# Score products of a windowed attention, in tiles of 104 and 64 key columns

## The chip, the cores and the metric

The kernel runs on one core of a Trainium2 chip. The time is the device time of one execution in microseconds (us); of several timed executions the median is given. The profile is of one execution more, taken by the hardware profiler.

## The reference

Four batches, eight heads, 768 positions and a head width of 64. Each position attends to the 96 positions up to and including itself and to the first 8 positions of its sequence, with a bias that falls with distance, by a slope of the head's own. The 512 numbers that the heads give for a position go through two projections to 1536, whose products are projected back to 512.

```python
scores = scale * np.matmul(q, k.transpose(0, 1, 3, 2))
rel = pos[:, None] - pos[None, :]
keep = (pos[None, :] < n_global) | ((rel >= 0) & (rel < n_local))   # 8 and 96
scores = np.where(keep, scores + bias, -1e9)
a = softmax(scores)                       # float32, as everything here
x = np.matmul(a, v)                       # then (B * S, H * D) = (3072, 512)
return ((x @ w_a) * (x @ w_b)) @ w_out    # (512, 1536) twice, (1536, 512)
```

## The kernel before, in words

**Tiling.** The 3072 rows are cut into six units of 512 rows (four blocks of 128 queries). Attention of a unit is done in four granules, each with four entries of two heads by one block. So there are 24 granules. `granule_ops` (line 547) does one: it loads `qk`, which holds queries and keys of the granule with the head's 64 numbers on the partitions, head 0 on partitions 0 to 63 and head 1 on 64 to 127, and does two rounds of two entries each. A round is one call of `scores` (line 574). It fills two PSUM banks, `ps[0]` for head 0 and `ps[1]` for head 1, with 2 x 168 columns: for each of the two entries 128 queries by 168 keys.

**Which keys.** The 128 queries of a block are taken as two halves, s = 0 and s = 1, of 64. For an entry the keys lie in `qk` as 232 columns (`KB`): columns 0 to 63 are positions -96 to -33 from the block's start, 64 to 159 are -32 to 63, 160 to 167 are the eight first positions of the sequence, and 168 to 231 are 64 to 127. Both halves need columns 64 to 167: that is 104 (`KX`). Half 0 also needs columns 0 to 63, and half 1 also 168 to 231. So each half has 168 keys (`KW`), of which the 104 shared ones come first in PSUM.

**The score products.** A matmul here has 64 partitions of input (one head's width) and 64 output lanes (one half), so it uses a quarter of TensorE's array. `tile_position=(64 * h, 64 * s)` says which: the head picks the rows, the half the columns. In the kernel before, `scores` issues for each entry, in this order and each for head 0 and then head 1: half 1 with all of its 168 columns (64 to 231 lie in a row), half 0 with the 104 shared ones, and half 0 with its own 64. These are six matmuls an entry, twelve a round, all recorded at line 581. The operands are float32.

**What follows a round.** For each entry and head VectorE adds the mask and takes the row's minimum (line 602), ScalarE takes the exponential and the sum (line 619), then come the division, the transposes and, a granule or so later, the value products (`values`, line 695, matmuls at line 701, `pa`). In three of the six units the values of a granule are computed during the next granule.

**The projections.** These are the bulk of TensorE's work: `product` and `plain_product` (lines 922 and 943, banks `al` and `ga`) and `back` (line 1099, banks `acc0` to `acc3`), with 512- or 256-column matmuls on the whole array, each product in three parts of a split of the numbers. Weights come in as 64-bit words and are converted on the chip (`to32`, line 351). The projections run over passes, a set of weights by a unit; the attention of later units is spread over the passes of earlier ones (`SPANS`, line 58).

**What sets the order.** Every piece of work is an `Op` with a due time and a cost for each engine that can do it. `Schedule.order` (line 176) walks through them like a list scheduler and fixes, before the program runs, the order of the instructions on every engine and of the transfers on SyncE's queue. A round of score products is one such `Op`, with a cost of 720 ns on TensorE (`pe=720`, line 591); what is due at its side is interleaved with it round by round, and not inside a round. Waits are between whole buffers: the mask operations of a round wait for the last matmul into their bank.

Of the kernel before, what the change touches and what calls it, by code (L numbers as in the profile page):

```python
# [34 lines left out]
KX = 96 + NG  # L35
KW = KX + 64
# [60 lines left out]
QUADS1 = (28400.0, 31000.0, 36000.0, 35540.0, 46130.0, 44380.0)  # L97
QUADS2 = (48000.0, 51000.0, 54000.0, 51210.0, 58890.0, 63000.0)
GAP = 20220.0


def entry(u, g, i):
    if u:
        return g, i
    return 2 * (g % 2) + i // 2, 2 * (g // 2) + i % 2
# [51 lines left out]
class Schedule:  # L157
# [14 lines left out]
    def op(self, due, emit, reads=(), writes=(), late=0.0, port=(), **costs):  # L172

        self.ops.append(Op(len(self.ops), due, costs, emit, reads, writes, late, port))
# [95 lines left out]
def act(n, psum=False):  # L270
    return (51 if psum else 93) + 0.833 * n


def dve(n, fast=False):
    return 67 + (0.523 if fast else 1.045) * n
# [14 lines left out]
class Fast:  # L290
# [256 lines left out]
    def granule_ops(self, u, p, due, x, d, before):  # L547
        nc, op = self.nc, self.plan.op
        n = f"{u}_{p}"
        g = self.granule  # L550
        self.granule += 1
        px, py = self.px[g % PTBUFS], self.py[g % PTBUFS]
        qk = self.kept("qk%d" % (g % KBUFS), "qk" + n)
        vt = self.sbuf([P, VN], F32, "vt", "vt" + n, VBUFS)
        if g >= KBUFS:
            self.dma(
                due - LOADLEAD,
                lambda: qk[:, :],
                lambda: self.a["qk"][u, p],
                [],  # L560
                [qk],
                (QN + KN) * 4 * P,
            )
        self.dma(
            due + VLAG - 4000.0, lambda: vt[:, :], lambda: self.a["vd"][u, p], [], [vt], VN * 4 * P
        )
        t = self.sbuf([P, NH, 2, KW], F32, "t", "t" + n, TBUFS)
        sm = self.sbuf([P, 4, 2 * NH], F32, "sm", "sm" + n, 3)
        for r in range(2):
            self.count += 1  # L570
            tags = self.early_bank("psS", u, p, self.count)
            ps = [self.bank(tags[h], f"ps{n}_{r}_{h}") for h in range(2)]

            def scores(e, r=r, ps=ps):
                for b in range(2):
                    i = 2 * r + b
                    q0, k0, c0 = i * P, QN + i * KB, b * KW
                    for s, c, k, w in ((1, 0, 64, KW), (0, 0, 64, KX), (0, KX, 0, 64)):
                        for h in range(2):
                            rows = slice(64 * h, 64 * h + 64)  # L580
                            nc.tensor.matmul(  # L581
                                ps[h][64 * s : 64 * s + 64, c0 + c : c0 + c + w],
                                qk[rows, q0 + 64 * s : q0 + 64 * s + 64],
                                qk[rows, k0 + k : k0 + k + w],
                                start=True,
                                stop=True,
                                skip_group_check=True,
                                tile_position=(64 * h, 64 * s),
                            )

            op(due, scores, [qk], ps, pe=720)
            for b in range(2):
                i = 2 * r + b
                pair, blk = entry(u, p, i)
                kind = 0 if (4 * u + blk) % NB == 0 else 1
                for h in range(2):
                    j = 2 * i + h
                    w = slice(b * KW, b * KW + KW)
                    op(
                        due,  # L600
                        lambda e, i=i, w=w, h=h, b=ps[h], j=j, kind=kind, pair=pair: (
                            nc.vector.tensor_tensor_reduce(  # L602
                                t[:, i, h],
                                b[:, w],
                                self.mask[pair][:, h, kind],
                                -0.125,
                                3.0e38,
                                ALU.add,
                                ALU.min,
                                sm[:, 0, j : j + 1],  # L610
                            )
                        ),
                        [ps[h], (self.mask[pair], h)],
                        [(t, j), (sm, j)],
                        dve=dve(KW) + 10,
                    )
                    op(
                        due,
                        lambda e, i=i, h=h, j=j: nc.scalar.activation(  # L619
                            t[:, i, h],  # L620
                            t[:, i, h],
                            AF.Exp,
                            bias=sm[:, 0, j : j + 1],
                            scale=-1.0,
                            accum_out=sm[:, 1, j : j + 1],
                        ),
                        [],
                        [(t, j), (sm, j)],
                        act=act(KW) + 200,
                    )  # L630
        if before:
            before()
        tt = None
        if u not in DIRECT:
            tt = self.sbuf([P, 6, 2 * NH * 32], F32, "tt", "tt" + n, TTBUFS)
        for half in range(2):
            js = range(4 * half, 4 * half + 4)
            jw = slice(4 * half, 4 * half + 4)
            op(
                due,  # L640
                lambda e, jw=jw: nc.vector.tensor_scalar_add(sm[:, 2, jw], sm[:, 1, jw], 1e-9),
                [(sm, j) for j in js],
                [(sm, ("d", half))],
                dve=70,
            )
            op(
                due,
                lambda e, jw=jw: nc.vector.reciprocal(sm[:, 3, jw], sm[:, 2, jw]),
                [(sm, ("d", half))],
                [(sm, ("r", half))],  # L650
                dve=80,
            )
            flat = lambda: t[:, :].rearrange("p a b c -> p (a b) c")

            def norm(e, js=js, jw=jw):
                if e == "act":
                    for j in js:
                        nc.scalar.mul(flat()[:, j], flat()[:, j], sm[:, 3, j : j + 1])  # L658
                else:
                    for j in js:  # L660
                        nc.vector.tensor_scalar(
                            flat()[:, j], flat()[:, j], sm[:, 3, j : j + 1], None, op0=ALU.mult
                        )

            ts = [(t, j) for j in js]
            op(due, norm, [(sm, ("r", half))], ts, port=BOTH, dve=4 * dve(KW, True), act=4 * (act(KW) + 100))

            if u in DIRECT:
                for i in range(2 * half, 2 * half + 2):
                    self.direct(u, p, n, i, due, t, px, py)  # L670
                continue

            def turn(e, half=half):
                dst = tt[:, :].rearrange("p e (j k) -> p j e k", k=32)[:, 4 * half : 4 * half + 4]
                src = t[:, 2 * half : 2 * half + 2].rearrange("p a b c -> p (a b) c")
                for e0, c0, n in ((0, 0, 4), (4, KX, 2)):
                    nc.vector.transpose(  # L677
                        dst[:, :, e0 : e0 + n],
                        src[:, :, c0 : c0 + 32 * n].rearrange("p j (e k) -> p j e k", e=n),
                    )  # L680

            op(due, turn, ts, [(tt, half)], dve=dve(512) + dve(256))
        if u not in DIRECT:
            self.carry(n, due, tt, px, py)

        def late():
            self.values(u, p, due, vt, px, py, x, d)

        return late
# [478 lines left out]
    def run(self):  # L1168
# [31 lines left out]
        for i, (stay, u) in enumerate(PASSES):  # L1200
# [27 lines left out]
            for k, fp in enumerate(fps):  # L1228
                due = t + k * (times[i + 1] - t) / len(fps)
                if not i:  # L1230
                    due = [h + k * GAP for h in (HALF0, HALF1)]
                parts = (self.project_plain if plain else self.project)(i, fp, due, xf[u])
# [369 lines left out]
```

## Time and profile before

| | |
|---|---|
| median of 3 timed runs | 725.11 us |
| lowest and highest | 724.22 and 725.52 us |
| the profiled execution's own time | 728.68 us |
| its span, from first to last instruction | 726.4 us |
| mean granted clock of TensorE | 0.987 |
| VectorE busy | 578.9 us (80%) |
| ScalarE busy | 387.7 us (53%) |
| VectorE, mask operation of line 602 | 192 of 326 ns |
| HBM read and written | 110.45 and 50.86 MB |

How to read the profile: PE is TensorE's products, PEld its weight loads, which run beside products; DVE is VectorE, ACT is ScalarE, SPq the queue of SyncE that issues transfers. Busy time of a group of instructions is the time in which at least one of them ran, so that four matmuls on four quarters of the array count once. A product's record begins where it may start and ends, by a model, when its last result has left the array; records of neighbours therefore overlap. The mean of one at line 581 is 278 ns, while 1152 of them take 43.6 us together. A float32 matmul of the scores or the values leaves two records of products and two of weight loads.

### The profile page before, as it was taken

The numbers are of one execution on the slowest core, as the hardware profiler recorded it, in microseconds if no ns is written. First come the engines' busy times: TensorE is split into PE (matmuls) and PEld (weight loads), VectorE is DVE, ScalarE is ACT, GpSimd is POOL, SyncE is SP. The second block draws the span as 40 slices with busy tenths as digits, with TensorE's granted clock in tenths as the row PEclk, the third lists the DMA queues.
The fourth block names the chain that finished last, engine by engine and source line by source line (L and its number), as shares of the span: only waits on it lengthen the run. The fifth ranks groups of instructions, "written<-read, shape, count | busy, mean of one in ns | idle before, by whom it ended". The sixth has DMA issues, their size and how long they took to land.

```text
span 726.4 us, 15134 instructions
## 1 busy us (share of the span) xinstructions
PE 693.5 (95%) x5584; PEld 605.8 (83%) x5584; DVE 578.9 (80%) x1544; ACT 387.7 (53%) x989; POOL 1.8 (0%) x8
## 2 busy tenths in 40 slices
PE   5698998999999999999999999999999999999996
PEld 4487887777777788788899899899989999999995
DVE  7999997777687785799989898999999557746652
ACT  5987775745465673746455545666343434434310
POOL 1000000000000000000000000000000000000000
PEclk9799999999999999999999999999999999999999
DMA  8547998897989897776676888756794423343221
GB/s 296 213 163 259 269 294 300 267 305 250 304 280 303 253 335 247 262 266 228 221 249 232 294 259 301 245 201 230 233 337 151 146 59 102 131 145 102 74 73 62
DMA packets 67906, 162.39 MB, mean 224 GB/s; under 512 B 8432, under 2 KB 21872, under 8 KB 66032
## 3 DMA queue, kind: packets, MB, share of 16 engines
q1 hardware_dynamic: 67824, 161.34, 66.8%
q8 instruction: 46, 0.75, 0.4%
q14 instruction: 36, 0.29, 0.1%
HBM read 110.45 MB, written 50.86 MB: 222 GB/s over the span
## 4 chain that ended last, share of the span: by engine, by line
PE 68%; DMA 12%; DVE 11%; ACT 5%; issue 2%; SPq 1%; DVEq 0%; ACTq 0%
PE acc L1099 19%; PE al L922 16%; PE ga L922 12%; DMA wr<-wts 8%; PE ps L581 4%; PE pa L701 3%; ACT t L619 1%; DMA py<-mir 1%; DVE tt L677 1%; DMA X<-dx 1%; DVE t L602 1%; DVE wm L394 1%; ACT wm L369 1%; DVE wm L411 1%; SPq L323 1%
## 5 line engine op out<-in xcount | busy, mean ns | idle before, releaser
L1099 PE MATMUL acc<-w_O,hh 128*128 128x512 f32 x576 | 196.6, 400 | 0.0
L1099 PEld LDWEIGHTS acc<-w_O,hh 128*128 128x128 f32 x576 | 108.4, 188 | 25.1 <-issue 1.7
L1099 PE MATMUL acc<-w_O,hl 128*128 128x512 f32 x288 | 113.8, 395 | 0.4 <-DVE hl L342 0.3
L619 ACT ACTIVATE t<-t,sm 128x168 f32<-128x168 f32 x192 | 81.1, 424 | 20.2 <-DVE sm L602 20.0
L922 PE MATMUL al<-xf_T,w_S 128*128 128x256 f32 x576 | 76.8, 283 | 0.0
L922 PEld LDWEIGHTS al<-xf_T,w_S 128*128 128x128 f32 x576 | 72.2, 189 | 0.5
L332 ACT CAST hh<-h 128x512 fp32r<-128x512 f32 (+1 forms) x62 | 36.6, 592 | 50.2 <-DVE h L342 22.5
L1099 PEld LDWEIGHTS acc<-w_O,hl 128*128 128x128 f32 x288 | 54.3, 188 | 10.5 <-DVE hl L342 1.1
L581 PEld LDWEIGHTS ps<-qk 64*64 64x64 f32 x1152 | 36.3, 142 | 28.1 <-issue 14.2
L602 DVE CUSTOM_DVE_ANT_0 t<-ps,mask 128x168 f32<-128x168 f32 x192 | 53.3, 326 | 6.1 <-PE ps L581 5.6
L581 PE MATMUL ps<-qk 64*64 64x168 f32 (+2 forms) x1152 | 43.6, 278 | 14.4 <-DMA qk<-qk 7.0
L332 ACT COPY s<-al 128x512 f32<-128x512 f32 x47 | 27.5, 585 | 52.2 <-PE al L922 52.2
L369 ACT ACTIVATE wm<-wr 128x512 f32<-128x512 f32 x54 | 36.2, 670 | 34.7 <-DMA wr<-wts 25.2
L342 DVE TENSOR_TENSOR hl<-h,hh 128x512 fp32r<-128x512 f32 (+1 forms) x78 | 49.8, 642 | 5.2 <-ACT hh L332 4.9
L1031 DVE TENSOR_TENSOR s<-ga,s 128x512 f32<-128x512 f32 x48 | 32.8, 683 | 16.2 <-PE ga L922 16.0
L677 DVE STREAM_TRANSPOSE tt<-t 128x512 f32<-128x512 f32 x80 | 41.1, 552 | 0.8 <-ACT t L658 0.4
L404 ACT ACTIVATE wr<-wr 128x512 int32<-128x512 uint32 x54 | 36.2, 673 | 7.2 <-DMA wr<-wts 4.3
L701 PE MATMUL pa<-px,vt 104*64 104x128 f32 x384 | 38.9, 278 | 1.2 <-DMA px<-mir 1.2
L922 PE MATMUL ga<-xf_B,w_S 128*128 128x256 f32 x288 | 38.6, 283 | 1.3 <-ACT s L332 1.3
L922 PEld LDWEIGHTS al<-xf_B,w_A 128*128 128x128 f32 x288 | 37.5, 189 | 2.3 <-issue 0.3
L922 PE MATMUL ga<-xf_T,w_S 128*128 128x256 f32 x288 | 38.6, 283 | 0.6 <-DVE s L1031 0.5
L701 PE MATMUL pa<-py,vt 128*64 128x128 f32 x384 | 38.0, 273 | 1.1 <-DMA py<-mir 1.0
(274 smaller groups left out, 1318.6 us busy)
## 6 DMA issues: line engine op xcount, KB each, us to landing
wr<-wts SPq DMA_DIRECT2D x54, 512.0 KB
qk<-qk SPq DMA_DIRECT2D x24, 720.0 KB
mir<-tt SPq DMA_DIRECT2D x20, 768.0 KB
vt<-vd SPq DMA_DIRECT2D x24, 512.0 KB
X<-dx SPq DMA_DIRECT2D x10, 1024.0 KB
part<-o SPq DMA_DIRECT2D x32, 256.0 KB
wl_S<-dw_S SPq DMA_DIRECT2D x32, 256.0 KB
px<-mir SPq DMA_DIRECT2D x60, 128.0 KB
```

Source lines behind the costliest of these rows:

```text
L332: self.nc.scalar.copy(out(), src())
L342: lambda e: self.nc.vector.tensor_tensor(out(), a(), b(), op=op),
L369: lambda e: nc.scalar.activation(m(), high().bitcast(F32), AF.Abs),
L404: lambda e: nc.scalar.activation(low(), low().bitcast(U32), AF.Copy, scale=2.0**-29),
L581: nc.tensor.matmul(ps[h][64 * s : 64 * s + 64, c0 + c : c0 + c + w], qk[rows, q0 + 64 * s : q0 + 64 * s + 64], qk[rows, k0 + k : k0 + k + ...
L602: nc.vector.tensor_tensor_reduce(t[:, i, h], b[:, w], self.mask[pair][:, h, kind], -0.125, 3.0e38, ALU.add, ALU.min, sm[:, 0, j : j + 1],)
L619: lambda e, i=i, h=h, j=j: nc.scalar.activation(t[:, i, h], t[:, i, h], AF.Exp, bias=sm[:, 0, j : j + 1], scale=-1.0, accum_out=sm[:, 1, j ...
L677: nc.vector.transpose(dst[:, :, e0 : e0 + n], src[:, :, c0 : c0 + 32 * n].rearrange("p j (e k) -> p j e k", e=n),)
L701: nc.tensor.matmul(pa[64 * h : 64 * h + 64, i * P : i * P + P], vt[:lanes, v0 : v0 + 64], k[:, :, 2 * i + h], start=c == 0, stop=c == 1, s ...
L922: self.nc.tensor.matmul(bank[:, ab * HT : ab * HT + HT], w[:, a, (2 * ab + c) * P : (2 * ab + c) * P + P], x[:, b, c], start=first, stop=F ...
L1031: lambda e: nc.vector.tensor_tensor(s[:, :], bank[:, :], s[:, :], op=ALU.add),
L1099: self.nc.tensor.matmul(acc[i][:, :], a[:, rows], w[:, b], start=first and f == 0 and k == 0, stop=False, skip_group_check=True,)
```

## The change

The two long matmuls of half 1 are cut in two: 104 shared columns and 64 of its own, like half 0's. A table `TILES` has the eight matmuls of an entry in the order of issue: first the 104 shared columns of the four tiles (half 0 head 0, half 0 head 1, half 1 head 0, half 1 head 1), then the 64 of the four in the same order. Each entry of the table is (half, head, first column in PSUM, first key column, width). So an entry has eight matmuls, and a round sixteen. The cost that the scheduler is told stays 720 ns.

```diff
+TILES = [(s, h, 0, 64, KX) for s in range(2) for h in range(2)]
+TILES += [(s, h, KX, (0, KW)[s], 64) for s in range(2) for h in range(2)]
...
                     q0, k0, c0 = i * P, QN + i * KB, b * KW
-                    for s, c, k, w in ((1, 0, 64, KW), (0, 0, 64, KX), (0, KX, 0, 64)):
-                        for h in range(2):
-                            rows = slice(64 * h, 64 * h + 64)
-                            nc.tensor.matmul(
-                                ps[h][64 * s : 64 * s + 64, c0 + c : c0 + c + w],
-                                qk[rows, q0 + 64 * s : q0 + 64 * s + 64],
-                                qk[rows, k0 + k : k0 + k + w],
+                    for s, h, c, k, w in TILES:
+                        rows = slice(64 * h, 64 * h + 64)
+                        nc.tensor.matmul(
+                            ps[h][64 * s : 64 * s + 64, c0 + c : c0 + c + w],
+                            qk[rows, q0 + 64 * s : q0 + 64 * s + 64],
+                            qk[rows, k0 + k : k0 + k + w],
...
             op(due, scores, [qk], ps, pe=720)
```

More of the change, by code (lines that the diff above doesn't have):

```diff
@@ L577, in scores @@
                     q0, k0, c0 = i * P, QN + i * KB, b * KW
-                    for s, c, k, w in ((1, 0, 64, KW), (0, 0, 64, KX), (0, KX, 0, 64)):
-                        for h in range(2):
-                            rows = slice(64 * h, 64 * h + 64)
-                            nc.tensor.matmul(
-                                ps[h][64 * s : 64 * s + 64, c0 + c : c0 + c + w],
-                                qk[rows, q0 + 64 * s : q0 + 64 * s + 64],
-                                qk[rows, k0 + k : k0 + k + w],
[L585 to L589, printed above, removed]
+                    for s, h, c, k, w in TILES:
[4 more added lines that the diff above has]
+                            qk[rows, k0 + k : k0 + k + w],
+                            start=True,
+                            stop=True,
+                            skip_group_check=True,
+                            tile_position=(64 * h, 64 * s),
+                        )
             op(due, scores, [qk], ps, pe=720)
```

## The prediction

> **What bounds the kernel now.** I read the page first, then the chain of waits with its shares by line, then the sums by stage, and last one score step start by start.
>
> ```profile
> span 726.4 us, 15134 instructions
> PE 693.5 (95%) x5584; PEld 605.8 (83%) x5584; DVE 578.9 (80%) x1544; ACT 387.7 (53%) x989; POOL 1.8 (0%) x8
> ```
>
> ```profile
> by line: PE acc L1099 19.3%; PE al L922 15.6%; PE ga L922 12.0%; DMA wr<-wts 7.8%; PE ps L581 3.6%; PE pa L701 3.4%; issue 1.6%; ACT t L619 1.5%; DMA py<-mir 1.2%; DVE tt L677 1.1%; DMA X<-dx 1.0%; DVE t L602 1.0%; DVE wm L394 0.9%; ACT wm
> ```
>
> TensorE is busy for 95% of a span of 726.4 us. In the shares by line (the head of the chain of waits) the score products, L581, hold 3.6%: 0.036 x 726.4 = 26.2 us. That is all that the change touches. The next fence has two stages with every instruction, then the last stage with L581 alone (each engine's busy us and instructions, PE and PEld first; at the end the clock, the DMA share and GB/s).
>
> ```profile
> 150.00:250.00 100.00, 98.11 (x800) 76.80 (x797) 76.35 (x247) 57.68 (x167) 0.00 (x0) 1.00 0.88 286
> 350.00:500.00 150.00, 148.93 (x1299) 135.23 (x1298) 136.51 (x345) 83.93 (x208) 0.00 (x0) 1.00 0.77 256
> ...
> 500.00:726.40 226.40, 0.00 (x0) 0.00 (x0) 1.00 0.41 135
> ```
>
> From 150 to 250 us TensorE is busy for 98.1 of 100 us, from 350 to 500 for 148.9 of 150, at full clock, so a score step there stands in a queue that has next to no holes. After 500 us there are no score products. So a longer or shorter score step is paid, or earned, one for one wherever it lies on the chain.
>
> How many do? L581 has 1152 product records:
>
> ```profile
> L581 PE MATMUL ps<-qk 64*64 64x168 f32 (+2 forms) x1152 | 43.6, 278 | 14.4 <-DMA qk<-qk 7.0
> ```
>
> Each step (one call of `scores`, two query blocks) issues 2 x 3 x 2 = 12 matmuls, and 24 granules x 2 rounds = 48 steps make 576; 1152 records are two for each matmul. I call such a record a pass. A step is thus 24 passes, and on the chain it is one piece:
>
> ```profile
> 231.33 0.75 PE ps L581 x16
> 232.08 2.97 PE al_0(0, 1)_2962 L943 x12
> ```
>
> Here it is 0.75 us, followed at once by the next group of products. 26.2 / 0.75 = 35 of the 48 steps lie on the chain; the other 13 end while something else is late. 35 is my multiplier throughout.
>
> One step in detail, the one at 231.26 us:
>
> ```profile
> 231.26 0.68 PEld L581 LDWEIGHTS ps<-qk 64*64 64x64 f32 x24 [0.37 <-issue]
> 231.26 0.82 PE L581 MATMUL ps<-qk 64*64 64x168 f32 x24
> 232.01 0.30 PEld L943 LDWEIGHTS al_0(0, 1)_2962<-xp,w_A 128*128 128x128 f32 x2
> 232.15 0.33 DVE L602 CUSTOM_DVE_ANT_0 t<-ps,mask 128x168 f32<-128x168 f32 x1
> ```
>
> Its first weight load and its first product start at 231.26, its products are over at 232.08 (231.26 + 0.82), the next group's first load starts at 232.01, which is the 0.75 us of the chain, and the mask operation on VectorE starts at 232.15, after the whole step.
>
> **The passes inside the step.** The next view is a count: stretches that all begin at 231.25 and end later and later, so (x) is the number of passes that have started by the end of each. I put most ends between the two starts of a pair (the two heads h), hence the odd counts.
>
> ```profile
> 231.25:231.29 0.04, 0.03 (x4) 1.00 0.98 205
> 231.25:231.42 0.17, 0.16 (x5) 1.00 0.48 120
> 231.25:231.46 0.21, 0.20 (x7) 1.00 0.47 117
> 231.25:231.51 0.26, 0.25 (x9) 1.00 0.46 126
> 231.25:231.56 0.32, 0.30 (x11) 1.00 0.38 104
> 231.25:231.60 0.35, 0.34 (x13) 1.00 0.37 105
> 231.25:231.62 0.37, 0.36 (x15) 1.00 0.44 133
> 231.25:231.72 0.47, 0.45 (x17) 1.00 0.51 159
> 231.25:231.75 0.49, 0.48 (x19) 1.00 0.59 174
> 231.25:231.80 0.55, 0.54 (x21) 1.00 0.64 201
> 231.25:231.86 0.61, 0.60 (x23) 1.00 0.64 208
> ```
>
> By 231.46 they are of these shapes:
>
> ```profile
> L581 PE MATMUL ps<-qk 64*64 64x168 f32 x3 | 0.5, 336 | 0.0
> L581 PE MATMUL ps<-qk 64*64 64x104 f32 x4 | 0.4, 274 | 0.0
> ```
>
> So the four tiles of the array (two query halves s, two heads h) all start within 0.04 us, and from there each tile goes its own way. By 231.46 half 0 has begun its second 104-column pass (x5) ahead of half 1's second 168-column pass (x7). From here on the code's order gives the rest. Half 0 starts at 0.42 (104), 0.51 and 0.56 (64), then in the second block 0.62 and 0.72 (104), 0.80 and 0.86 (64): a 104-column pass takes about 0.09 us, a 64-column one 0.05 to 0.06, and a whole block, 0.42 to 0.72, 0.30. Half 1 has two passes of 168 columns to a block: 0.46, 0.60, 0.75, so 0.14 to 0.15 each and about 0.29 a block. The two halves do equal columns (104 + 64 = 168) in nearly equal time, side by side. Half 0 is the later by 0.01 or so a block, and the step ends with its last 64-column pass.
>
> **The change part by part.**
>
> *Removed:* two matmuls of 168 columns a block (half 1). *Added in their place:* two of 104 and two of 64. A step goes from 12 to 16 matmuls, from 24 to 32 passes, and has as many weight loads more, 8. Columns, results, banks and every other engine's instructions stay as they are. The order in which steps are issued stays too, since the planner is still told 720 ns for a step; no DMA and no queue is moved past another.
>
> *Half 1's time.* It now has half 0's sequence, 104, 104, 64, 64, which the trace prices at 0.30 a block. It goes from 0.29 to 0.30, and still ends beside half 0 and not behind it. Half 0's own sequence is unchanged. Cover for the added passes: half 0 itself, which the step waits for in any case. If the cover were gone, 0.01 a block, 0.02 a step, would show: 35 x 0.02 = 0.7 us.
>
> *The place in the order.* Now half 0's pair is issued first and half 1's second. The last tile to start is still the fourth of four within 0.04 us, and the last pass is still a 64-column one. Only the half differs, and whether it leaves the array later can be read from the value products, which end on the upper output half:
>
> ```profile
> 229.12 0.39 PE L701 MATMUL pa<-px,vt 104*64 104x128 f32 x4
> 229.34 0.39 PE L701 MATMUL pa<-py,vt 128*64 128x128 f32 x4
> ...
> 229.46 0.27 PE L701 MATMUL pa<-py,vt 128*64 128x128 f32 x1
> 229.66 0.50 PE L1099 MATMUL acc<-w_O,hh 128*128 128x512 f32 x1
> ...
> 231.85 0.23 PE L581 MATMUL ps<-qk 64*64 64x64 f32 x2
> ```
>
> Four passes (two tiles, two each) start every 0.22 us, 229.12 to 229.34, so one takes 0.11. The last starts at 229.46 and the next group at 229.66: 0.20 - 0.11 = 0.09 of emptying. The score step ends on the lower half: last pair at 231.85 to 231.86, its pass 0.06, the next group at 232.01, again 0.09 to 0.10. No difference, so 0.
>
> *The eight added weight loads.* This is the operation that the trace shows only in part: four tiles that need new weights at the same moment, again and again, where now half 1's loads fall between half 0's. The nearest rows are the start of the step (loads alone, counted as above):
>
> ```profile
> 231.25:231.31 0.06, 0.05 (x4) 1.00 0.65 137
> 231.25:231.32 0.07, 0.06 (x5) 1.00 0.56 117
> 231.25:231.34 0.09, 0.08 (x8) 1.00 0.44 91
> ```
>
> Four loads are out by 0.31 and all eight by 0.34, that is, the second set of four follows the first after 0.05 to 0.06 and itself takes 0.03 or less to get under way. The second passes then start when the first ones' columns are through (0.09 and 0.14), not when a load is. So four loads at a time cost nothing behind a 104-column pass. Behind a 64-column one, 0.05 to 0.06 long, the margin is nearly nil: a load comes every 0.05 to 0.06 in a tile. Bounds: below, half 0 at half 1's rate a column, 0.29 a block, -0.02 a step, -0.7 us. Above, the loads take turns in pairs and a 64-column pass needs 0.11; a tile has four such passes in a step, 4 x 0.055 = 0.22 a step, +7.7 us. I take 0, because the set of four at the step's start got under way within 0.03, half of a 64-column pass.
>
> [...]
>
> *Waits.* The first matmul of a step waits for its bank, and the rest is queued behind it, before and after. VectorE waits for the end of the step:
>
> ```profile
> DVE t L602 <- PE ps L581: 5.6, 13, 1.1
> ```
>
> 13 waits of 5.6 us in all; they move with the step's end, so by nothing. If the second head's bank is late, the first head's first tile runs on and all others wait, in both orders, with two blocks of one half still to come.
>
> *Code.* The instruction queue:
>
> ```profile
> q8 instruction: 46, 0.75, 0.4%
> ```
>
> 384 more passes and 384 loads on 15134 instructions are 5% more of a queue at 0.4% of the DMA engines: nothing.
>
> *Sum:* 35 x 0 = 0. The profiled execution took 728.68 us, its span 726.4 and 2.3 outside it; it stays at 728.7. That run lies 3.6 us above the median of the three timed runs, 725.11 (724.22 to 725.52), which carry no profile, and I give the forecast on that scale: **725.1 us, no change**. About 0.2%, 1.45 us, is what a measurement of this kernel can tell from no change; with 35 steps that is 0.041 us a step, or 0.010 on each of the four 64-column passes of a tile.
>
> **Rivals.**
>
> *Slower: the four tiles' loads collide in the 64-column passes.* Place: two passes of each block in which all four tiles are in step. For it: the pass (0.05 to 0.06) is no longer than the distance of two loads in a tile, and in the kernel before only two tiles are ever in such passes together. Against: the set of four at the start. Price: 0.22 a step at the far end, 35 x 0.22 = 7.7, 732.8 us; with a quarter of that, 0.055 a step, 1.9 us and 727.0. It decides from 0.010 a pass. Chance of over 0.2% by it 0.15, more of it near 727 than near 733.
>
> *Slower: the array starts passes at a fixed rate, whatever the tile.* For it: 24 passes start in 0.60 us (231.26 to 231.86), 0.025 each; at that rate 32 passes take 0.80, +0.20 a step, 7.0 us, 732.1 us. Against: four start within 0.04, and the later starts of each tile lie at distances that go by its own columns (0.09, 0.055, 0.14). Chance 0.04. [...]
>
> *Faster: half 1's long passes hold half 0 back.* For it: half 0's block takes 0.30, half 1's 0.29 for the same columns; in the second block the 104-column pass from 0.62 to 0.72 looks longer than the one after it (0.72 to 0.80). Against: a tile with four passes a block has two starts more than one with two, and this would stay. Price: at most -0.02 a step, 724.4 us, which is still within 0.2%. To be faster by more, a shift of the steps would have to shorten the waits for DMA further on, for which I see no row. Chance of over 0.2%, with the scatter of two medians: 0.14.
>
> **How the numbers follow.** No change to within 0.2%: 0.66, from 723.7 to 726.6. Slower 0.20: 0.15 and 0.04 from the two rivals, and the scatter. Faster 0.14. The range is to hold 8 in 10: below it takes half of the faster cases, to 723.2; above, the near part of the collisions, to 727.4 (0.065 a step). Outside lie the far ends at 732 to 733 and the tails.
>
> **What would show it.** In the profile of the changed kernel L581 has 1536 passes, 32 a step, and a step on the chain is still 0.75. In the count by start, taken from a step's first load: 4 by 0.03, 8 by 0.18, 12 by 0.27, 16 by 0.32, 20 by 0.38, 32 by 0.62. Pairs become fours. If the collisions are real, the steps to 16, to 20 and to 32 come later by over 0.01 each and the 0.75 grows; if the fixed rate is real, 32 comes at 0.80. The half that ends last would show as wrong if the emptying after the last pass is not 0.09. Wrong altogether I would be if the step keeps 0.75 and the time still moves by over 1.5 us: then the number of steps on the chain, or what follows them, was misread.

## The result and the profile after

The changed kernel is slower: a median of 730.26 us of twelve runs (726.30 to 732.39) against 725.83 us for the kernel before beside it, a ratio of 1.0064 with a 95% interval of 1.0039 to 1.0089. All ratios here are estimated from the single runs of both kernels, leaving out those in the slow state, so they need not be the quotients of the medians given. One of the twelve runs of the kernel before took 2328.69 us; without it their median is 725.52. The forecast was 725.1 us and no change; its range ended at 727.4. The profiled execution took 731.96 us, its span 729.8. The page of the changed kernel (lines of code are three higher in it than before, L584 for L581, L925 for L922):

```profile
span 729.8 us, 15902 instructions
...
PE 692.5 (95%) x5968; PEld 605.1 (83%) x5968; DVE 579.0 (79%) x1544; ACT 388.4 (53%) x989; POOL 1.8 (0%) x8
...
q8 instruction: 49, 0.80, 0.4%
```

There are 768 more instructions than the 15134 of before. TensorE's busy time is 692.5 us where it was 693.5, so the work has not become longer. What has grown is the rest of the span: 729.8 - 692.5 = 37.3 us without TensorE, against 726.4 - 693.5 = 32.9. The 4.4 us are waits. (In a second profile of the kernel before, `null` below, the same rest is 723.6 - 690.1 = 33.5 us.)

The score products themselves, first their sum on the page, then one step in the chain of waits, then that step's start by start (columns as before, counted from a window that begins 0.01 us ahead of the first load):

```profile
L584 PE MATMUL ps<-qk 64*64 64x104 f32 (+1 forms) x1536 | 43.5, 250 | 13.9 <-DMA qk<-qk 7.1
```

```profile
229.85 0.75 PE ps L584 x32
230.60 2.97 PE al_0(0, 1)_3086 L946 x12
```

```profile
229.77:229.81 0.04, 0.03 (x4) 1.00 0.50 205
...
229.77:230.09 0.32, 0.30 (x15) 1.00 1.01 416
...
229.77:230.40 0.63, 0.62 (x32) 1.00 1.01 416
```

L584 is busy for 43.5 us where it was 43.6 us with 1152 passes, and a step on the chain is 0.75 us with 32 passes as it was with 24. Four passes start within 0.03 us of the first load at 229.78, the 15th by 0.31 and the 32nd by 0.62. Nothing of the loss lies in the step that was changed.

It lies later. Here is the chain of waits of the changed kernel from 392 to 403 us, from the second half of the run:

```profile
393.61 6.32 DMA wr<-wts
...
400.03 0.07 ACT wr L408
...
400.58 0.58 ACT s L336
...
401.21 1.69 PE al L925 x12
```

A weight transfer `wr<-wts`, issued at 393.61, lands 6.32 us later, and a chain of ScalarE work hangs on it. In the kernel before, the transfer is issued at 394.90, and the chain of the same stretch is all TensorE:

```profile
392.49 5.58 PE acc L1099 x24
398.06 1.42 PE al L922 x12
399.48 1.42 PE ga L922 x12
400.90 1.43 PE al L922 x12
```

The timeline shows who waits for whom. First the kernel after, then the kernel before (in square brackets the idle time ahead of it and what ended that):

```profile
396.60 1.59 PE L925 MATMUL al<-xf_B,w_A 128*128 128x256 f32 x12
...
400.03 0.66 ACT L408 ACTIVATE wr<-wr 128x512 int32<-128x512 uint32 x1 [5.40 <-DMA wr<-wts]
...
400.58 0.57 ACT L336 COPY s<-al 128x512 f32<-128x512 f32 x1
...
401.21 1.46 PE L925 MATMUL al<-xf_T,w_S 128*128 128x256 f32 x10 [1.60 <-ACT s L336]
```

```profile
394.90 0.38 SPq L363 DMA_DIRECT2D wr<-wts  x1
...
397.90 1.59 PE L922 MATMUL al<-xf_B,w_A 128*128 128x256 f32 x12
...
398.89 0.68 ACT L404 ACTIVATE wr<-wr 128x512 int32<-128x512 uint32 x1 [2.97 <-DVE o L1134]
...
399.52 0.59 ACT L332 COPY s<-al 128x512 f32<-128x512 f32 x1
...
400.74 0.52 PE L922 MATMUL al<-xf_T,w_S 128*128 128x256 f32 x3
```

Both kernels run the same order: the product group `al<-xf_B`, the conversion of the weights on ScalarE (L408, before L404), the copy `s<-al` on ScalarE, the product group `al<-xf_T`. The copy empties the bank that `al<-xf_T` writes, and ScalarE does the conversion first, so a late transfer holds the copy and the copy holds TensorE. At `al<-xf_B` the changed kernel is 1.30 us ahead (396.60 against 397.90). At `al<-xf_T` it is 0.47 us behind (401.21 against 400.74). These 1.77 us are lost in one place, 1.6 of them as idle time of TensorE, and the score step is not near it.

The same kind of wait is longer over the whole span. These are the rows of the waits for weights, after and then before (us in all, times, longest):

```profile
ACT wm L373 <- DMA wr<-wts: 27.6, 18, 4.5
...
ACT wr L408 <- DMA wr<-wts: 9.0, 4, 5.4
```

```profile
ACT wm L369 <- DMA wr<-wts: 25.2, 17, 4.6
...
ACT wr L404 <- DMA wr<-wts: 4.3, 2, 3.1
```

36.6 us against 29.5, or 32.5 with the wait of 2.97 us shown for L404 above, which is put down to VectorE and ends with the transfer as well. In the second profile of the kernel before these rows come to 33.2, so about half of the growth is no more than two executions of one kernel differ by. ScalarE is busy for 53% of the span and has room to idle, so not all that these waits grow by reaches TensorE.

### The profile page after: what moved, and what is told of

The parts are those of the page before. It is cut to its first block, busy times and chain, and to the rows that moved or that the text cites. A ratio compares the mean times of both kernels' runs of the same rounds, so it can differ in the third digit from the quotient of the medians.

```text
span 729.8 us, 15902 instructions
## 1 busy us (share of the span) xinstructions
PE 692.5 (95%) x5968; PEld 605.1 (83%) x5968; DVE 579.0 (79%) x1544; ACT 388.4 (53%) x989; POOL 1.8 (0%) x8
## 4 chain that ended last, share of the span: by engine, by line
PE 67%; DVE 17%; DMA 11%; ACT 2%; issue 2%; SPq 0%; DVEq 0%; ACTq 0%
PE acc L1102 21%; PE al L925 14%; PE ga L925 10%; DMA wr<-wts 4%; PE pa L704 4%; PE ps L584 3%; DMA o<-part 2%; DMA out<-o 2%; DVE t L605 2%; DVE wm L415 1%; DVE t L664 1%; DVE s L1034 1%; DVE wm L398 1%; DVE tt L680 1%; DVE hl L346 1%
## 5 line engine op out<-in xcount | busy, mean ns | idle before, releaser
L925 PE MATMUL al<-xf_T,w_S 128*128 128x256 f32 x576 | 77.4, 284 | 3.4 <-ACT s L336 3.4
L925 PEld LDWEIGHTS al<-xf_T,w_S 128*128 128x128 f32 x576 | 72.7, 190 | 4.3 <-ACT s L336 3.8
L336 ACT CAST hh<-h 128x512 fp32r<-128x512 f32 (+1 forms) x62 | 36.6, 592 | 52.2 <-DVE h L346 21.3
L584 PEld LDWEIGHTS ps<-qk 64*64 64x64 f32 x1536 | 36.3, 142 | 27.4 <-issue 14.1
L584 PE MATMUL ps<-qk 64*64 64x104 f32 (+1 forms) x1536 | 43.5, 250 | 13.9 <-DMA qk<-qk 7.1
L408 ACT ACTIVATE wr<-wr 128x512 int32<-128x512 uint32 x54 | 36.1, 673 | 9.0 <-DMA wr<-wts 9.0
L925 PE MATMUL ga<-xf_T,w_S 128*128 128x256 f32 x288 | 38.9, 285 | 1.5 <-DVE s L1034 1.5
L925 PEld LDWEIGHTS al<-xf_B,w_A 128*128 128x128 f32 x288 | 37.5, 188 | 2.3 <-issue 0.3
L925 PEld LDWEIGHTS ga<-xf_T,w_S 128*128 128x128 f32 x288 | 37.1, 191 | 2.8 <-DVE s L1034 1.7
```

The lines of the kernel that those rows point to most:

```text
L336: self.nc.scalar.copy(out(), src())
L408: lambda e: nc.scalar.activation(low(), low().bitcast(U32), AF.Copy, scale=2.0**-29),
L584: nc.tensor.matmul(ps[h][64 * s : 64 * s + 64, c0 + c : c0 + c + w], qk[rows, q0 + 64 * s : q0 + 64 * s + 64], qk[rows, k0 + k : k0 + k + ...
L925: self.nc.tensor.matmul(bank[:, ab * HT : ab * HT + HT], w[:, a, (2 * ab + c) * P : (2 * ab + c) * P + P], x[:, b, c], start=first, stop=F ...
```

## The experiments

Three theories were open after the result. **Order or shape:** the eight matmuls an entry, in their new order, disturb what follows the step. **Code:** the 768 further instructions (384 passes and 384 loads) cost something although the step hides them. That one again came in two forms, by the amount of code or by where its pieces are fetched. **Arrival:** the step is equal, and small shifts draw other waits for DMA in each execution. In what follows a "further record" is one such instruction.

**The kernels again.** First the scatter, with the two kernels unaltered.

> The changed kernel once more, unaltered. In its profile a score step keeps its 0.75 us on the chain and yet the time was 4.4 us longer. Code theory (192 more matmul instructions cost something wherever they stand): again 729 to 731 us, +0.4 to +0.9%. Order theory (which half starts and ends costs): the same. Arrival theory (the step is equal, and small shifts draw other waits for DMA in each execution): +0.2 to +0.9%, and a second profile puts the lost time at other places than the first did. If it comes out within 0.2%, the first difference was the scatter of executions.

> The kernel before, unaltered, timed against itself. All theories: within 0.2%, 723.5 to 728 us. Its second profile shows how far two executions of one program differ in their waits for DMA: under the arrival theory the start of the same products differs by 2 us or more at places, under the code theory by under 0.5 us.

The changed kernel gave 732.62 us beside 726.17, a ratio of 1.0097 (1.0071 to 1.0123). The kernel before, measured as if it were new, gave 726.39 us, 1.0016 (0.9987 to 1.0045). So a true "same" looks like that, and the loss repeats, a little above the range expected for it.

The second profiles speak to arrival. In `null` the same products start up to 3.5 us earlier than in the first profile of the same kernel (2.0 us earlier at 390 us), so a single execution differs from the next by nearly as much as the loss, as that theory said. But it also said that a second profile of the changed kernel would lose its time at other places, and `again` has the wait near 400 us once more (1.79 us, for 0.12 in `null`). Arrival is real scatter in one execution; it does not by itself explain medians that differ each time the changed kernel is run.

**Cut and order apart.** `split` keeps the order of before and only cuts half 1's matmul:

```diff
-for s, c, k, w in ((1, 0, 64, KW), (0, 0, 64, KX), (0, KX, 0, 64)):
+for s, c, k, w in ((1, 0, 64, KX), (1, KX, KW, 64), (0, 0, 64, KX), (0, KX, 0, 64)):
```

> Only the cut: half 1's 168 columns are cut into 104 and 64 where they stood, so 16 matmuls a step, half 1 first as before. Code theory: slower by 0.4 to 0.9%, 729 to 731 us. Order theory: within 0.2%, 724.5 to 727. Arrival theory: anywhere from -0.4 to +0.9% with a step of 0.75 us.

`order0` keeps the six matmuls an entry and issues half 0's 104 columns first:

```diff
-for s, c, k, w in ((1, 0, 64, KW), (0, 0, 64, KX), (0, KX, 0, 64)):
+for s, c, k, w in ((0, 0, 64, KX), (1, 0, 64, KW), (0, KX, 0, 64)):
```

> Only the order: still 12 matmuls a step, but half 0's 104 columns first, then half 1's 168, then half 0's 64. Code theory: within 0.2%, 724.5 to 727 us. Order theory: slower by 0.4 to 0.9%, 729 to 731. Arrival theory: anywhere from -0.4 to +0.9% with a step of 0.75 us.

`split` took 731.01 us, 1.0073 (1.0043 to 1.0102). `order0` took 726.63 us, 0.9998 (0.9974 to 1.0022). Order alone costs nothing that could be measured; the loss comes with the cut and its 768 further records. One step of each in its chain of waits, first `split`, then `order0` (x30 and x19 count the pieces of the chain; the steps have 32 and 24 passes):

```profile
229.89 0.80 PE ps L581 x30
```

```profile
227.66 0.73 PE ps L581 x19
```

The split step is longer, 0.80 us against 0.75. By the multiplier of 35 that is 35 x 0.05 = 1.75 us, a third of its loss, so `split` is no clean test of code. The step of `order0` is shorter by 0.02 us at most, 35 x 0.02 = 0.7 us, which no measurement here can tell from nothing.

**Code without a change of the step.** The next kernels leave the step as it is and put one-column matmuls that nobody reads ahead of the first step; each makes four records, two loads and two passes (16 of them left 32 loads and 32 passes of `pad` in `before_pad64`).

```diff
+for i in range(N):
+    nc.tensor.matmul(pad[lanes, 512 * h : 512 * h + 1], ident[rows, lanes],
+                     ident[rows, :1], ..., tile_position=(64 * h, 64 * s))
 main.run()
```

Where do the pieces of code lie? The queue "instruction" of the profile holds 46 pieces in the kernel before and 49 in the changed one: 0.80 MB / 49 = 16 KB a piece, and 768 further records for three pieces are 256 records each. TensorE's own records before, 2 x 5584 = 11168, would be 44 such pieces, near the 46, so by these counts I take this for the queue of TensorE's code. (A second queue of this kind, q14, has 36 pieces of 8 KB in both kernels, and in none of the profiles a piece from 380 to 420 us.) Then, by my estimate from these counts, 128 further records (N = 32) move the later fetches of TensorE's code by half a piece, and 256 by a whole one, which brings the fetches back to the same places of the work. If the amount is what costs, at (730.26 - 725.83) / 768 = 5.8 ns a record, 128 records cost 0.7 us, 0.10%. If the place is what costs, 128 cost as much as 768, and 256 nothing.

> The kernel before, with 32 one-column matmuls (128 records on TensorE) ahead of its first score step, where TensorE waits for its first keys; they write a bank that nobody reads. Nothing else is changed. Amount theory (each further instruction costs, 5 us on 768 records): +0.8 us at most, 726 to 727 us. Fetch theory (the instruction queue brings TensorE's code in 16 KB pieces, and a piece that falls beside a transfer that the path waits for delays it): every later piece is fetched half a piece, some 8 us, earlier; one that stood at 404.9 us comes near 396, as in the changed kernel, the weight transfer issued near 394 lands after 7.8 instead of 6.5 us, the 12 products al<-xf_T,w_S after it wait 1.8 us instead of 0.1, and the time is 2 to 6 us longer, 728 to 732.

> The changed kernel with the same 32 one-column matmuls (128 records) ahead of its first step. Amount theory: no faster than the changed kernel, 730 to 733 us. Fetch theory: near 395 us the count of further records is then 640 + 128 = 768, three whole pieces, so the fetches stand near 388 and 405 as in the kernel before, the wait of 1.8 us before the products al<-xf_T,w_S near 400 us is gone, and the time is 1.5 to 5 us shorter than the changed kernel's, 726 to 730.

> The kernel before with 16 one-column matmuls (64 records) ahead of its first step. Amount theory: +0.4 us, within 0.2%. Fetch theory: fetches come a quarter of a piece, some 4 us, earlier, at other places than in any kernel so far; the time lies anywhere between 724 and 732 us, and where it is longer a wait for a transfer stands beside a fetch.

> The changed kernel with 48 one-column matmuls (192 records) ahead of its first step. Amount theory: 731 to 733 us. Fetch theory: near 450 us the further records are 704 + 192 = 896, three and a half pieces, near 395 us 832, three and a quarter; the time lies anywhere between 724 and 733 us, and not by the number of added instructions.

The figures of 6.5 and 7.8 us in the expectations came from a count of landings in which some records were missing; by a transfer's own sixteen landings they are 3.9 and 6.3, as used here.

- `before_pad128`: 730.96 us beside 725.70, 1.0056 (1.0017 to 1.0094).
- `after_pad128`: 730.44 us beside 725.70, 1.0044 (1.0015 to 1.0074).
- `before_pad64`: 727.54 us beside 725.70, 1.0022 (0.9990 to 1.0053).
- `after_pad192`: 731.57 us beside 725.70, 1.0092 (1.0061 to 1.0123).

The kernel before, with its step untouched, loses with 128 records nearly what the change loses with 768. The changed kernel does not get its time back with 128 more records, although its wait near 400 us is gone, as its chain there shows:

```profile
393.64 5.57 PE acc L1102 x24
399.21 1.42 PE al L925 x12
400.64 1.42 PE ga L925 x12
402.06 1.43 PE al L925 x12
```

So the place was foretold, and the total was not: it was to be 1.5 to 5 us shorter than the changed kernel's. `before_pad64` can't be told from no change.

**Half a piece by the change itself, and a whole piece by padding.** Padding also delays the first step, from 7.0 us to 7.5, 7.7 and 9.4 with 64, 128 and 256 records in the kernel before. So `cut_first8` makes its 128 further records by the change, in the first 8 of 48 steps, and `before_pad256` (N = 64) adds a whole piece, with the longest delay of all. The other two split the change in two halves of 384 records:

```diff
+for s, h, c, k, w in TILES if 2 * g + r < 8 else WHOLE:    # cut_first8
+for s, h, c, k, w in TILES if 2 * g + r < 24 else WHOLE:   # cut_early
+for s, h, c, k, w in TILES if 2 * g + r >= 24 else WHOLE:  # cut_late
```

`WHOLE` holds the six matmuls of before.

> The change in the first 8 score steps alone, all over by 42 us; the other 40 are the kernel before's. 128 further records instead of 768. Amount theory: a sixth of the change's cost, +0.8 us, 726 to 727. Fetch theory: all code after 42 us is fetched half a piece early, as with the 128 records put ahead of the first step, now without holding up that step; a fetch stands at 395 to 398 us, the wait of over 1 us before the products al<-xf_T,w_S near 400 us is there, and the time is 728 to 732 us, most of what the whole change costs.

> The kernel before with 64 one-column matmuls, 256 records, one whole 16 KB piece, ahead of its first step, which they hold up by some 2 us at a time when the path is elsewhere. Amount theory: +1.7 us. Theory that the pad itself harms by holding up the start: more than the 128 records did, over 731 us. Fetch theory: all later fetches stand where the kernel before has them, no wait before the products al<-xf_T,w_S near 400 us, and the time is back at 725 to 727.5 us.

> The change in the first 24 score steps alone, over by 192 us, 384 further records, one and a half pieces. Amount theory: +2.5 us, 728. Fetch theory: from 192 us on the phase is half a piece off, as in the changed kernel near 395 us; the wait of over 1 us near 400 us is there though no step after 192 us is changed; 728 to 732 us.

> The change in the last 24 score steps alone, from 191 us on. Amount theory: +2.5 us, 728. Fetch theory: up to 190 us as the kernel before; near 395 us 16 changed steps have passed, 256 records, one whole piece: no wait near 400 us. 725 to 729 us.

- `cut_first8`: 730.64 us beside 727.55, 1.0068 (1.0037 to 1.0099).
- `before_pad256`: 727.51 us beside 727.55, 1.0008 (0.9983 to 1.0032).
- `cut_early`: 732.64 us beside 727.55, 1.0078 (1.0045 to 1.0111), 0.64 us above the range expected.
- `cut_late`: 730.54 us beside 727.55, 1.0071 (1.0039 to 1.0104).

128 further records cost 0.68% and 256 cost nothing that can be measured. A cost by amount (0.10% for 128, 0.31% for 384) lies below the intervals of all three cut kernels and of `before_pad128`. Taken from the dearest measurement of the change, 0.97%, it would be 0.16% for 128, still below both intervals, but 0.49% for 384, which lies in them; so the two kernels with 128 decide. The 256 fit the theory of the place, but they don't decide: by amount they would cost 0.20%, which lies in the interval of `before_pad256`, and that interval meets the one of `before_pad128` from 0.17 to 0.32%. A delayed start by itself does not explain the loss, since `before_pad256` has the longest. `cut_late` is a miss in its total: its records stand at a whole piece near 395 us, the wait there is gone as foretold, and they cost as much as the others all the same.

**One place, compared in all profiles.** It is the transfer `wr<-wts` near 394 us. A transfer lands in sixteen parts, each with a signal of its own. The table is worked out from the trace's record of these signals; times are us after the issue, and the last column runs from the start of the product ahead to the start of the first product of `al<-xf_T` after it (0.12 where nothing is waited for).

| kernel (after is the changed one) | further records by then, over whole pieces | 15th part | 16th part | code fetch beside it, at us | TensorE |
|---|---|---|---|---|---|
| before | 0 | 3.85 | 3.88 | none | 0.12 |
| null | 0 | 3.65 | 3.67 | none | 0.12 |
| order0 | 0 | 3.77 | 3.93 | none | 0.12 |
| before_pad256 | 0 | 3.85 | 3.95 | none | 0.12 |
| cut_late | 0 | 4.00 | 4.05 | none | 0.12 |
| after_pad128 | 0 | 3.73 | 4.22 | none | 0.12 |
| before_pad64 | 64 | 4.07 | 4.21 | none | 0.12 |
| after_pad192 | 64 | 4.21 | 4.28 | none | 0.12 |
| after | 128 | 3.71 | 6.32 | 395.15 | 1.88 |
| again | 128 | 4.45 | 6.24 | 397.57 | 1.79 |
| split | 128 | 3.96 | 6.28 | 394.46 | 1.85 |
| before_pad128 | 128 | 4.05 | 5.75 | 395.16 | 1.32 |
| cut_first8 | 128 | 4.13 | 5.67 | 392.20 | 1.24 |
| cut_early | 128 | 3.91 | 5.99 | 399.52 | 1.54 |

Fifteen parts land after 3.7 to 4.5 us in all fourteen kernels. Where a piece of code is fetched beside the transfer, the sixteenth comes 1.5 to 2.6 us behind them, and TensorE waits 1.2 to 1.9 us. Where none is, it doesn't. Which kernel is of which kind goes by the further records by then, less whole pieces, and not by whether the step is cut.

At the other transfers `wr<-wts` the link is weaker. In the fourteen profiles there are 402 more whose sixteen signals can be told apart. With a code fetch that starts in the first 3 us after the issue, the sixteenth part comes over 1 us behind the fifteenth in 12 of 64; with no fetch from 1 us before the issue to the landing, in 13 of 221. So a late part is more frequent beside a fetch, a fetch does not always bring one, and parts are late without it as well.

The fetch is in the rows of the DMA queues; here the changed kernel from 394 to 398 us, then `cut_first8` from 390 to 394:

```profile
q8 instruction: 1, 0.02, 1.4%
```

```profile
q8 instruction: 1, 0.02, 2.1%
```

In the kernel before, that queue has no row from 390 to 402 us; its fetches are one in 386 to 390 and one in 402 to 406. The chains read accordingly, first `cut_first8`, then `before_pad256`:

```profile
391.52 5.67 DMA wr<-wts
...
397.30 0.07 ACT wr L409
...
397.86 0.58 ACT s L337
...
398.49 1.58 PE al L926 x11
```

```profile
392.46 5.58 PE acc L1099 x24
398.04 1.42 PE al L922 x12
399.46 1.42 PE ga L922 x12
400.88 1.43 PE al L922 x12
```

Eight steps of the change, over long before (the 448 passes of the first 16 steps had all started by 101.5 us), bring the late transfer, and a whole piece of code leaves the chain as it was before.

**Where the total comes from.** The mean start of the same product in after, again and split, less that in before, null and order0, is +0.85 us until some 398 us, +2.68 at 408, +2.70 at 443, +4.46 at 458 and +3.97 at the end. The first jump, 1.8 us, is the place above. Of the second, 1.4 of 1.8 us are a wait of the same kind at 457 us behind another weight transfer; the changed kernel's chain there:

```profile
448.72 6.91 DMA wr<-wts
...
457.41 0.47 ACT s L336
...
457.93 2.23 PE al L925 x12
```

In the changed kernel and in `again` a code fetch starts within 0.02 us of that issue, and the transfer takes 6.91 and 7.17 us. In `split` one starts 0.29 us after it, and the transfer takes 5.55, as in before (5.52), with a wait of TensorE of 0.35 us against 2.1 and 2.3. So a fetch beside a transfer does not always delay it. Nor is a fetch needed there: `after_pad128`, `cut_early` and `cut_first8` wait 1.50, 1.59 and 1.08 us at the same product with no code fetch beside that transfer. And the transfers of 6.91 and 7.17 us are late as a whole, with the last part only 0.41 and 0.57 us behind the fifteenth. So the second place is not shown to be of the first one's kind.

The waits of the whole span sort the kernels better than any one place. Those that the profile puts down to `wr<-wts` come to 29.5 to 35.2 us in the five kernels whose time can't be told from the kernel before's (before, `null`, `order0`, `before_pad64`, `before_pad256`) and to 36.5 to 45.6 in the nine slower ones. That the loss is made of such waits fits this; what lengthens them outside the first place is not shown. The profiled executions, one for each kernel, also scatter (that of `before_pad64` took 723.4 us, its median is 727.5), so they tell the place and the medians tell the price.

## Why the prediction was wrong

**The step was right, and not by luck.** 1536 passes, 0.75 us, all six counts by start (from 4 by 0.03 to 32 by 0.62), no half that holds up the other.

**Order and emptying were right.** The last pass starts 0.60 us after the first load, as before, and the next group's first load comes 0.75 after it:

```profile
229.78 0.68 PEld L584 LDWEIGHTS ps<-qk 64*64 64x64 f32 x32 [0.37 <-issue]
...
230.53 0.30 PEld L946 LDWEIGHTS al_0(0, 1)_3086<-xp,w_A 128*128 128x128 f32 x2
```

`order0` measures half 0's pair first by itself: 0.9998.

**The rivals of the step were rightly put low.** Colliding loads would have lengthened the step by up to 0.22 us, a fixed rate of starts by 0.20; it grew by nothing. In the changed kernel 32 passes on tiles of 64 by 64 started in 0.62 us, 0.019 each; at the 0.025 of the kernel before (24 in 0.60 us) they would have taken 0.80.

**The step that failed is the paragraph "Code".** It read "q8 instruction: 46, 0.75, 0.4%", worked out 5% more of a queue that takes 0.4% of the DMA engines, and set the cost to nothing. With it goes the sentence that no queue is moved past another. But 0.4% is the mean over the span. The piece that mattered is one of 16 KB beside one transfer of 512 KB in sixteen parts, of which the slowest counts, 6.3 us after the issue for 3.9. TensorE waited 1.2 to 1.9 us for it, against 0.12 without a fetch. And the number of further pieces was not what cost: 128 records cost 0.56 and 0.68% with no piece more (46 in both), and 256, a piece more, nothing that could be measured (1.0008). What the added instructions are seen to do is move the fetches of TensorE's code against the data transfers: near this place the kernel before has them at 388.4 and 404.9 us, the changed one at 383.3 and 395.2. That this makes up the whole loss, and not only the part at this place, is not shown. The prediction asked for each queue what was added to it and not what was moved past what.

TensorE is not seen to wait for code at the score steps: the idle time that the profile can't put down to anything ("issue") is 14.1 us ahead of their weight loads, for 14.2 before. What was late is the data transfer near 394 us, by one of its sixteen parts, with a piece of code beside it. Why that part is late is not shown: it is 1.5 to 2.6 us late where the piece itself takes 0.88 to 1.35, and the trace does not record which of the sixteen engines fetched.

**"Wrong altogether"** was foreseen for a step of 0.75 us and a time that moves all the same, and the fault was to lie in the number of steps on the chain or in what follows them. The number doesn't matter for a step that costs the same. What follows was it, as far as the loss was found: a wait for `wr<-wts`, behind which ScalarE's queue holds the copy that frees TensorE's bank.

**What stays open.** The second place near 457 us; why one fetch delays a part and another doesn't; why `split` takes longer for its step; why `after_pad128` and `cut_late`, free of the late part near 394 us, still lose 0.44 and 0.71%; and how the sum over all transfers comes out for a given shift, which would have to be known to foretell a time. A version without the fetch, or with the code in another queue, wasn't tried. No version was faster than the kernel before.

## What to carry to other kernels

Here added instructions shifted the fetches of TensorE's code (near one place 388.4 and 404.9 us in the kernel before, 383.3 and 395.2 in the changed one), and 128 of them cost 0.6 to 0.7% and 256 nothing that could be measured, part of the cost at a place that the change doesn't touch; the row of the code queue, and the last of a transfer's parts, belong to the first things to read when the changed part is as fast as before. Before such a time is put down to the change, measure it beside the old kernel with some dead instructions that shift the code by half a piece and by a whole one. And a forecast of "no change" from a hidden edit wants a range that is wide enough for that shift, here about +0.7%.

## What the runs showed of the hardware

- The queue that by its counts holds TensorE's code moved pieces of 16 KB, 46 in the kernel before and 49 with 768 records more, so 256 records a piece. At one 512 KB transfer a piece beside it took 0.88 to 1.35 us, and the last of the transfer's sixteen parts landed 1.5 to 2.6 us after the fifteen others, in 6 kernels of 6, and within 0.5 us of them in the 8 without such a piece. At the other transfers it was over 1 us late in 12 of 64 with a piece beside it and in 13 of 221 without.
- On four 64 by 64 tiles of the array, four float32 passes, one on each, started within 0.03 us of the first load, and 32 passes of 104 and 64 columns, with 32 loads, by 0.62 us when they were issued four tiles at a time.
- One step of each kernel on its chain of waits took 0.80 us with the tiles cut but issued half after half, 0.75 in the order of the change, and 0.73 with six uncut matmuls and half 0's shared columns first (0.75 before).
